# First batch's keys and values loaded by tokens and pooled in four quadrants, scaled in the copy

## The chip, the cores and the metric

One core of a Trainium2 chip runs the whole program. The metric is the device time of one execution in microseconds (us). Three runs of the kernel before took 746.22, 747.27 and 748.57 us; the median is 747.27 us. Five engines work side by side, each through its own instructions in a fixed order: TensorE (PE; its weight loads are listed as PEld), VectorE (DVE), ScalarE (ACT), GpSimd (POOL) and SyncE (SP), which here only issues DMA transfers. They wait for each other through semaphores.

## What is computed

Memory attention over 4 batches, 8 heads, 576 tokens, 64 numbers a head and 32 memory slots, and two feed-forward layers behind it on the 2304 tokens:

```python
a = np.exp(phi - np.max(phi, axis=2, keepdims=True))
a = a / (np.sum(a, axis=2, keepdims=True) + 1e-09)        # over the 576 tokens
k_m = np.einsum('bhsm,bhsd->bhmd', a, k)                   # pooled keys, 32 a head
v_m = np.einsum('bhsm,bhsd->bhmd', a, v)                   # pooled values
scores = np.matmul(q, k_m.transpose(0, 1, 3, 2)) / np.sqrt(64)
attn = softmax(scores)                                     # over the 32 slots, with 1e-09
x = np.matmul(attn, v_m)                                   # then heads side by side: 2304 x 512
x = (x @ w_a) * (x @ w_b) @ w_out                          # 512 -> 1536 -> 512
h = x @ w2_in
return np.maximum(0.01 * h, h) @ w2_out                    # 512 -> 2048 -> 512
```

## The kernel before, in words

The pooled values are never multiplied with the attention by themselves. Instead v_m is multiplied with a piece of w_a and w_b (`plan_w`, TensorE line L1195, written to the PSUM tile `wp`), the result is split into a high and a low part W (ACT L1220, DVE L1224), and the attention AT, also split (ACT L1135, DVE L1139), is multiplied with W in three passes (`plan_ab`, L1257, tile `ab`). ACT copies the a half (L1274), DVE multiplies it with the b half (L1279), the product G is split (L1294, L1298), and `plan_x1` multiplies it with w_out (L1323, tile `x1p`). Such a unit of work covers one batch and six of the twelve 128-wide column blocks f; there are eight units, four batches with f 0 to 5, then four with f 6 to 11. The second layer (lines L1761 and above, tiles `h` and `o`) starts when all is done, and its code and order are untouched by the change.

The weights arrive as 64-bit-like words through `stage` tiles, and each load of 512 KB is converted by ACT and POOL or ACT (L436, L440, L444) and joined by DVE (L454); w_out takes two more steps (ACT L462, DVE L465).

Batch 0 stands at the head of the program, where nothing can cover it. Its steps: maximum and exponential of phi into e; the pooling of keys and then values (`pool_pairs`, L754, 36 multiplications each, tile `km`); the sums of e over tokens (`total`, L799), their inverse r (L808, L809); the inverse spread to rows (`to_rows`, L816, and copies L826, L838); the pooled block copied out (L856, L859) and turned (`mem_t`, L870, tile `kvT`); the turned keys multiplied with the rows into kk (L886), the turned values multiplied with the rows into vblk (L894); queries turned (L1026, L982); the scores (L1062, L1068); and the softmax on DVE and ACT (row maximum L1005, subtraction L1014, exponential L1091, row sums L1100, inverse L1107, product L1112). The result is turned (L1122) and split into AT. Small multiplications without use (`warm`, L1691) keep TensorE at work in the gaps of the first 27 us.

The pooling of the keys multiplies, for token row j, the lower and the upper 64 partitions (g) with the heads of one half (a):

```python
out=km0[64 * a:64 * a + 64, g, 128 * n:128 * n + 128],
lhsT=c["e"][rows, j, 2 * a:2 * a + 2].rearrange("p q m -> p (q m)"),
rhs=c["kv", a][rows, :, n, D * j:D * j + D],
```

The order of all instructions up to the second layer comes from a planner (`Plan`): every step has an engine, a cost, the steps it waits for and a latest time, and the planner runs through the steps engine by engine, always taking the most urgent one that can start. A table of numbers (`SEEDS`) then shifts the latest times of randomly drawn steps, one draw for each number. So a change in a step's cost, in what it waits for, or in the table can move instructions anywhere up to the second layer. The ranks in `first` fix the order of the first twelve loads on SP.

Of the kernel before, what the change touches and what calls it, by code (L numbers as in the profile page):

```python
# [46 lines left out]
class Plan:  # L47
# [14 lines left out]
    SEEDS = (732418, 598209, 67790, 750449, 735046, 463859, 81198, 743086, 257381, 567596, 473366, 451655, 673169,  # L62
             737747, 770024, 60013, 601371, 972463, 52455, 949269, 18998, 526698, 544420, 584452, 460089, 892981,
             534221, 902381, 581733, 954758, 270819, 973106, 531934, 82330, 738265, 747344, 546437, 989455, 690754)
# [272 lines left out]
def kernel(  # L337
# [182 lines left out]
    att_all = []  # L520
# [8 lines left out]
    def plan_att(b):  # L529
# [15 lines left out]
        kv_slots = ((kv_before, kv_users), (early_end() if b >= B - 2 else [], []))  # L545
# [12 lines left out]
        for n, (name, src) in enumerate((("k", k), ("v", v))):  # L558
            ld_kv.append([])
            for i in range(2):  # L560
                part = slice(2 * i, 2 * i + 2)

                def load_kv(n=n, i=i, part=part, src=src):
# [5 lines left out]
                late = 0.5 if b == 0 and n and not i else 0.0  # L569
                ld_kv[n].append(add(DMA, 1.5 + late, load_kv, kv_slots[i][0], uses=[kv_slots[i][1]]))  # L570
# [94 lines left out]
        if b == 0:  # L665
# [23 lines left out]
            for i in range(2):  # L689

                def part_sum(i=i):
                    e = c["e"]
                    x = e[:, NR:] if i else e[:, 0:3]
                    dve.tensor_tensor(out=e[:, NR:], in0=x, in1=e[:, 3 * i + 3:3 * i + 6], op=ALU.add)

                s_es.append(add(DVE, t_dve(384), part_sum, s_exp[:i + 2] + s_es, port=True, uses=[e_users]))
        else:
            es_before, es_users = plan.slot("mx")
        for i in range(2 if b else 0):
# [17 lines left out]
            def part_sum(i=i):  # L717
# [5 lines left out]
                )  # L723

        for i in range(2 if b else 0):
            s_es.append(add(
                DVE, t_dve(384), lambda i=i: part_sum(i), s_exp + s_es + es_before, port=True, uses=[phi_users, es_users]
            ))
# [20 lines left out]
        def pool_pairs(n, a, j0, j1):  # L749

            for j in range(j0, j1):
                for g in range(NG):
                    rows = slice(D * g, D * g + D)
                    pe.matmul(  # L754
                        out=km0[64 * a:64 * a + 64, g, 128 * n:128 * n + 128],
                        lhsT=c["e"][rows, j, 2 * a:2 * a + 2].rearrange("p q m -> p (q m)"),
                        rhs=c["kv", a][rows, :, n, D * j:D * j + D],
                        start=j == 0, stop=j == NR - 1, skip_group_check=True,
                    )

        if b == 0:
            s_pool = []
            for n in range(2):
                end = []
                for a in range(2):
                    for i, (j0, j1) in enumerate(thirds):
                        end.append(add(
                            PE, POOL2 / 40 * NG * (j1 - j0), lambda n=n, a=a, j0=j0, j1=j1: pool_pairs(n, a, j0, j1),
                            [s_exp[i], ld_kv[n][a]] + sum(s_pool, []) + end[-1:] + r_before,
                            uses=[e_users, kv_users], n=4 * NG * (j1 - j0), kind="f",  # L770
                        ))
# [9 lines left out]
        if b == 0:  # L781
            t0_before = [plan.slot("t0", 2) for _ in range(NG)]
            t1_before, t1_users = plan.slot("t1")
            s_r, s_rv = [], []
            rm_before, rm_users = plan.slot(f"G{FH - 1}")

            def rows_place():
                c["rm"] = keep.tile([128, NG, NQ, 2, M], F32, tag=f"G{FH - 1}", name="rows")
                nc.gpsimd.memset(c["rm"], 0.0)

            s_rm = add(POOL, 0.5, rows_place, rm_before, uses=[rm_users])
            rv_before, rv_users = plan.slot("kmn")
            r_before, r_users = plan.slot("r")
            hold = Hold("ab", 2 + NG)
# [1235 lines left out]
```

## Time and profile before

| | |
|---|---|
| median of three runs | 747.27 us |
| the profiled execution | 745.72 us, of which 743.6 us are the span of its instructions |
| TensorE busy | 735.3 us, 99% of the span |
| VectorE, ScalarE, GpSimd busy | 579.3, 415.4, 17.9 us |
| first product of AT and W | starts 30.02 us into the span |
| second layer | first multiplication at 388.24 us |
| granted TensorE clock | nine tenths of full speed or more in all of the 40 slices |

The profiled execution was 1.55 us faster than the median of the runs. TensorE's busy time counts an instruction from its start to its modelled end, so a full share says that it always had something in it, and not that it did useful work: the fillers of the head count as busy. DMA share 1.00 and above means that all 16 transfer engines had work all the time.

### The profile page before, as it was taken

The numbers are of one execution on the slowest core, as the hardware profiler recorded it, in microseconds if no ns is written. First come the engines' busy times: TensorE is split into PE (matmuls) and PEld (weight loads), VectorE is DVE, ScalarE is ACT, GpSimd is POOL, SyncE is SP. The second block draws the span as 40 slices with busy tenths as digits, with TensorE's granted clock in tenths as the row PEclk, the third lists the DMA queues.
The fourth block names the chain that finished last, engine by engine and source line by source line (L and its number), as shares of the span: only waits on it lengthen the run. The fifth ranks groups of instructions, "written<-read, shape, count | busy, mean of one in ns | idle before, by whom it ended". The sixth has DMA issues, their size and how long they took to land.

```text
span 743.6 us, 14566 instructions
## 1 busy us (share of the span) xinstructions
PE 735.3 (99%) x5409; PEld 660.1 (89%) x5409; DVE 579.3 (78%) x1192; ACT 415.4 (56%) x917; POOL 17.9 (2%) x33
## 2 busy tenths in 40 slices
PE   9999999999999999999999999999999999999997
PEld 6798897987988888887999999999999999999986
DVE  5897685957917899998746766998866997877796
ACT  3786774765739687765514454644444743454441
POOL 1110000000300000000000000000000000000000
PEclk9999999999999999999999999999999999999999
DMA  9995366472804888777547787788898777878583
GB/s 313 352 370 177 106 242 215 156 238 77 268 7 165 270 319 301 253 258 284 194 161 227 264 247 256 253 254 251 256 299 285 262 250 244 280 226 312 150 301 86
DMA packets 86918, 175.28 MB, mean 236 GB/s; under 512 B 8000, under 2 KB 35136, under 8 KB 86848
## 3 DMA queue, kind: packets, MB, share of 16 engines
q1 hardware_dynamic: 86128, 173.77, 70.3%
q8 instruction: 43, 0.70, 0.4%
q10 hardware_dynamic: 720, 0.59, 0.3%
q14 instruction: 27, 0.22, 0.1%
HBM read 140.25 MB, written 34.08 MB: 234 GB/s over the span
## 4 chain that ended last, share of the span: by engine, by line
PE 96%; DVE 2%; DMA 1%; issue 0%; ACT 0%; SPq 0%
PE h L1761 24%; PE ab L1257 21%; PE x1p L1323 18%; PE o L1861 15%; PE o L1865 8%; PE wp L1195 3%; PE warm L1691 1%; PE km L754 1%; DMA stage<-in_moe_w_out_dram 1%; PE qT L1026 1%; PE sc L1062 1%; PE km L742 1%; PE aT L1122 1%; PE h L1836 0%; DVE s L1112 0%
## 5 line engine op out<-in xcount | busy, mean ns | idle before, releaser
L1861 PE MATMUL o<-w2o,S 128*128 128x512 f32 (+1 forms) x504 | 177.1, 387 | 0.0
L1257 PEld LDWEIGHTS ab<-AT,W 128*128 128x128 f32 x1152 | 154.6, 188 | 9.3 <-ACT W L1220 5.6
L1257 PE MATMUL ab<-AT,W 128*128 128x288 f32 x1152 | 160.8, 298 | 1.5 <-DVE W L1224 1.0
L1323 PE MATMUL x1p<-G,wo 128*128 128x512 f32 (+1 forms) x720 | 155.4, 371 | 0.3 <-DVE r L914 0.3
L1813 ACT ACTIVATE S<-g 128x384 fp32r<-128x384 f32 x168 | 87.6, 523 | 99.5 <-PE o L1861 86.0
L1323 PEld LDWEIGHTS x1p<-G,wo 128*128 128x128 f32 x720 | 123.7, 189 | 21.6 <-DVE r L914 0.6
L1761 PE MATMUL h<-T,ring 128*128 128x384 f32 x720 | 141.8, 335 | 0.0
L1865 PE MATMUL o<-w2o,S 128*128 128x256 f32 x492 | 137.6, 280 | 0.0
L1761 PEld LDWEIGHTS h<-T,ring 128*128 128x128 f32 x720 | 120.9, 188 | 4.1
L1814 DVE TENSOR_TENSOR S<-g,S 128x384 fp32r<-128x384 f32 x168 | 91.4, 553 | 40.4 <-ACT S L1813 40.2
L1861 PEld LDWEIGHTS o<-w2o,S 128*128 128x128 f32 x504 | 93.7, 188 | 14.6
L1865 PEld LDWEIGHTS o<-w2o,S 128*128 128x128 f32 x492 | 92.8, 189 | 0.0
L1883 DVE TENSOR_TENSOR C<-C,o 128x768 f32<-128x768 f32 x75 | 71.0, 948 | 13.9 <-ACT C L1887 7.9
L1761 PE MATMUL h<-B,ring 128*128 128x384 f32 x288 | 57.2, 336 | 0.0
L1804 DVE TENSOR_TENSOR g<-g 128x384 f32<-128x384 f32 x96 | 52.2, 552 | 2.9 <-ACT g L1771 2.4
L1761 PEld LDWEIGHTS h<-B,ring 128*128 128x128 f32 x288 | 48.8, 188 | 1.6
L436 ACT ACTIVATE stage<-stage 128x512 f32<-128x512 f32 x68 | 46.1, 683 | 4.1 <-DMA stage<-in_moe_w_in_dram 3.1
L1274 ACT COPY a_sb<-ab 128x288 f32<-128x288 f32 x96 | 37.3, 398 | 13.9 <-PE ab L1257 13.2
L1279 DVE TENSOR_TENSOR g<-a_sb,ab 128x288 f32<-128x288 f32 x96 | 42.3, 447 | 2.9 <-PE ab L1257 1.4
L1224 DVE TENSOR_TENSOR W<-wp,W 128x256 fp32r<-128x256 f32 (+1 forms) x75 | 35.1, 493 | 8.4 <-ACT W L1220 7.7
L1298 DVE TENSOR_TENSOR G<-g,G 128x576 fp32r<-128x576 f32 x48 | 37.1, 772 | 3.8 <-ACT G L1294 3.1
L1294 ACT ACTIVATE G<-g 128x576 fp32r<-128x576 f32 x48 | 33.1, 690 | 9.7 <-DVE g L1279 9.4
(146 smaller groups left out, 743.3 us busy)
## 6 DMA issues: line engine op xcount, KB each, us to landing
w2o<-a_scr SPq DMA_DIRECT2D x168, 256.0 KB, 3.7
ring<-a_scr SPq DMA_DIRECT2D x72, 512.0 KB, 4.4
stage<-in_moe_w_out_dram SPq DMA_DIRECT2D x28, 512.0 KB, 4.8
a_scr<-w2o SPq DMA_DIRECT2D x24, 512.0 KB, 4.4
a_scr<-a_out SPq DMA_DIRECT2D x24, 512.0 KB, 4.8
stage<-in_moe_w_in_dram SPq DMA_DIRECT2D x16, 512.0 KB, 5.2
stage<-in_moe_w_a_dram SPq DMA_DIRECT2D x12, 512.0 KB, 8.2
stage<-in_moe_w_b_dram SPq DMA_DIRECT2D x12, 512.0 KB, 8.2
```

Source lines behind the costliest of these rows:

```text
L436: act.activation(out=x, in_=x, func=ACTF.Prelu, scale=2.0 ** -112, alpha=2.0 ** 32)
L1257: pe.matmul(out=c[x, n][:, :HS], lhsT=W[b, f][:, hw, g, 128 * x:128 * x + 128], rhs=AT[b][:, g, ha, n * HS:(n + 1) * HS], start=(g == 0 an ...
L1274: act.copy(c["sb"][:, n], c[0, n][:, :HS])
L1279: dve.tensor_tensor(out=c["g"][:, n], in0=c["sb"][:, n], in1=c[1, n][:, :HS], op=ALU.mult)
L1323: pe.matmul(out=c["ps"], lhsT=wo_t[f][:, hw, 128 * m:128 * m + 128], rhs=G[f][:, hg, first:first + n], start=(f == fs[0] and (hw, hg) == P ...
L1761: pe.matmul(out=out, lhsT=ring[i % 2, part][:, o, kp, hw], rhs=x[:, hx], start=fresh and kp == 0 and (hw, hx) == PASSES[0], stop=kp == 1 a ...
L1804: dve.tensor_tensor(out=t, in0=x, in1=y, op=op)
L1813: act.activation(out=t[:, 0], in_=src, func=ACTF.Copy)
L1814: dve.tensor_tensor(out=t[:, 1], in0=src, in1=t[:, 0].bitcast(F32), op=ALU.subtract)
L1861: pe.matmul(out=dst[:, u, :y - x], lhsT=hi, rhs=wide[:, x:y], start=fresh and x == 0, stop=False, skip_group_check=True,)
L1865: pe.matmul(out=dst[:, u, :256], lhsT=lo, rhs=t[:, 0], start=False, stop=q == 3, skip_group_check=True,)
L1883: o_adds.append(lambda x=x: dve.tensor_tensor(out=total[name], in0=total[name], in1=x, op=ALU.add))
```

## The change

For batch 0, a load of keys or values used to bring two of the four head pairs with all nine token rows; it now brings all four head pairs with six token rows first (768 KB) and three after (384 KB). The pooling goes through all four quadrants (halves of heads a, halves of partitions g) for each token row. The second load of w for f 0 is put ahead of the values. DVE adds the three partial sums to one row, for all batches, so that the multiplication that sums over partitions is one in place of three. For batch 0, the inverse is no longer spread to rows: the copy of the pooled block scales with r, kk is multiplied with a mask of zeros and ones that POOL writes at the start, and vblk becomes a copy. `plan_w_parts` makes the products of a W whose halves lie in two banks wait for both halves in the plan (but for the first W). The table `SEEDS` has 53 numbers in place of 39.

```diff
-    SEEDS = (732418, 598209, 67790, 750449, 735046, 463859, 81198, 743086, 257381, 567596, 473366, 451655, 673169,
+    SEEDS = (683652, 560159, 530175, 125177, 433488, 159828, 165231, 686446, 405802, 158260, 349165, 253408, 67255,
...
+                def load_all(n=n, i=i, src=src):
+                    if ("kv", n) not in c:
+                        pool, tag = (keep, "AT1") if n else (p_att, "kv")
+                        c["kv", n] = pool.tile([128, NQ, NR * D], F32, tag=tag, name="kv_t")
+                    x = slice(6 * D * i, 6 * D + 3 * D * i)
+                    dma.dma_start(out=c["kv", n][:, :, x], in_=flat(src)[:, :, x])
...
-                late = 0.5 if b == 0 and n and not i else 0.0
-                ld_kv[n].append(add(DMA, 1.5 + late, load_kv, kv_slots[i][0], uses=[kv_slots[i][1]]))
+                if b == 0:
+                    late = 0.5 if n and not i else 0.0
+                    ld_kv[n].append(add(DMA, (2.0, 1.05)[i] + late, load_all))
+                else:
+                    ld_kv[n].append(add(DMA, 1.5, load_kv, kv_slots[i][0], uses=[kv_slots[i][1]]))
...
+                for j in range(1, 1 + 2 * i):
+                    dve.tensor_tensor(out=es[:, 0], in0=es[:, 0], in1=es[:, j], op=ALU.add)
...
             for j in range(j0, j1):
-                for g in range(NG):
-                    rows = slice(D * g, D * g + D)
-                    pe.matmul(
-                        out=km0[64 * a:64 * a + 64, g, 128 * n:128 * n + 128],
-                        lhsT=c["e"][rows, j, 2 * a:2 * a + 2].rearrange("p q m -> p (q m)"),
-                        rhs=c["kv", a][rows, :, n, D * j:D * j + D],
-                        start=j == 0, stop=j == NR - 1, skip_group_check=True,
-                    )
+                for a in range(2):
+                    for g in range(NG):
+                        rows = slice(D * g, D * g + D)
+                        pe.matmul(
+                            out=km0[64 * a:64 * a + 64, g, 128 * n:128 * n + 128],
+                            lhsT=c["e"][rows, j, 2 * a:2 * a + 2].rearrange("p q m -> p (q m)"),
+                            rhs=c["kv", n][rows, 2 * a:2 * a + 2, D * j:D * j + D],
+                            start=j == 0, stop=j == NR - 1, skip_group_check=True,
+                        )
...
-                for j in range(3):
-                    pe.matmul(
-                        out=c["sum"][:, :NG], lhsT=c["e"][:, NR + j].rearrange("p q m -> p (q m)"), rhs=ones,
-                        start=j == 0, stop=j == 2,
-                    )
...
+                pe.matmul(
+                    out=c["sum"][:, :NG], lhsT=c["e"][:, NR].rearrange("p q m -> p (q m)"), rhs=ones, start=True, stop=True
+                )
...
+                    for i in range(NG if n else 1):
+                        src = km0[:, g + i, 128 * n:128 * n + 128].rearrange("p (u d) -> p u d", u=2)
+                        dst = t[:, :, i] if n else t
+                        src = src if n else src.unsqueeze(2).to_broadcast([128, 2, 2, D])
+                        scale = c["r"][:, 1, g + i:g + i + 1]
+                        if on == ACT:
+                            act.activation(out=dst, in_=src, func=ACTF.Copy, scale=scale)
+                        else:
+                            dve.tensor_scalar(out=dst, in0=src, scalar1=scale, scalar2=None, op0=ALU.mult)
...
-                        dve.tensor_tensor(out=kk[g], in0=src, in1=c["rm"][:, g], op=ALU.mult)
+                        dve.tensor_tensor(out=kk[g], in0=src, in1=c["mask"], op=ALU.mult)
...
-                        dve.tensor_tensor(out=vblk[b], in0=c["kvT", 0, 1], in1=c["rv"], op=ALU.mult)
+                    def values(copy):
+                        copy(vblk[b], c["kvT", 0, 1])
...
-            for g in range(NG) if wide else (k,):
-                w_end[b, f, g] = [hi, lo]
+            ends = [hi, lo] if k == 0 or (b, f) == (0, 0) else ends + [hi, lo]
+            for g in (k,) if (b, f) == (0, 0) else range(NG):
+                w_end[b, f, g] = ends
...
-        ("wab", 0, 0), ("v", 0, 0), ("wab", 0, 1), ("v", 0, 1), ("wab", 1, 0), ("wab", 1, 1),
+        ("wab", 0, 0), ("wab", 0, 1), ("v", 0, 0), ("v", 0, 1), ("wab", 1, 0), ("wab", 1, 1),
```

The lines of the changed kernel have other numbers: L754 becomes L771, L799 L814, L870 L858, L1026 L1014, L982 L970, L1195 L1183, L1257 L1246, L1323 L1312, and ACT's L436, L856 and L1220 become L438, L844 and L1208.

On TensorE, from the pooling of the keys (`km`) to the last step ahead of the scores, before:

```order
L754 MATMUL km<-kv_t,e 64x128 x30
L799 MATMUL sum<-ones,e 128x2 x3
L754 MATMUL km<-kv_t,e 64x128 x6
L1026 MATMUL qT<-ident,q_t 128x128 x4
L816 MATMUL sum<-ident,r 128x128 x2
L870 MATMUL kvT<-ident,kc 128x2x32 x4
L982 MATMUL qL<-ident,q_t 128x128 x2
L1026 MATMUL qT<-ident,q_t 128x128 x8
```

and now:

```order
L771 MATMUL km<-kv_t,e 64x128 x36
L814 MATMUL sum<-ones,e 128x2
L1014 MATMUL qT<-ident,q_t 128x128 x4
L858 MATMUL kvT<-ident,kc 128x2x32 x4
L1014 MATMUL qT<-ident,q_t 128x128 x4
L970 MATMUL qL<-ident,q_t 128x128 x2
L1014 MATMUL qT<-ident,q_t 128x128 x4
L970 MATMUL qL<-ident,q_t 128x128 x2
```

The sums stand behind all of the pooling, the two multiplications that spread r are gone, and twelve turns of queries stand between the turned keys (kvT) and the first score, all of the second queries' among them.

On ScalarE, from the copy of the pooled values (kc) to the first attention parts (AT), before; `stage` is the conversion of a weight load:

```order
L856 COPY kc<-km 128x256
L440 ACTIVATE stage<-stage 128x512
L436 ACTIVATE stage<-stage 128x512
L440 ACTIVATE stage<-stage 128x512
L436 ACTIVATE stage<-stage 128x512
L1135 ACTIVATE AT<-aT 128x3x2x64
L1220 ACTIVATE W<-wp 128x256 x2
L1135 ACTIVATE AT<-aT 128x3x2x64 x2
```

and now:

```order
L844 ACTIVATE kc<-km,r 128x2x64 x2
L438 ACTIVATE stage<-stage 128x512
L882 COPY vblk<-kvT 128x128
L438 ACTIVATE stage<-stage 128x512
L1208 ACTIVATE W<-wp 128x256 x2
L1123 ACTIVATE AT<-aT 128x3x2x64 x2
```

ScalarE now makes vblk itself, between the conversions of the two weight loads for f 1 (the second waits for the load of w_b), and the first W and all of AT stand behind that second conversion.

On TensorE in the first unit, from the second pair's W products (`wp`) on; `ab` are products of AT and W, `x1p` those of G and w_out, `km` the pooling of batch 1. Before:

```order
L1195 MATMUL wp<-wab,vblk 32x512 x8
L625 MATMUL mxT<-ident,mx 128x128
L1257 MATMUL ab<-AT,W 128x288 x3
L1026 MATMUL qT<-ident,q_t 128x128 x4
L1257 MATMUL ab<-AT,W 128x288 x6
L655 MATMUL bc<-ident,gx 128x128
L1257 MATMUL ab<-AT,W 128x288 x30
L982 MATMUL qL<-ident,q_t 128x128 x4
L1257 MATMUL ab<-AT,W 128x288 x15
L1026 MATMUL qT<-ident,q_t 128x128 x4
L1257 MATMUL ab<-AT,W 128x288 x3
L1323 MATMUL x1p<-G,wo 128x512 x3
```

and now:

```order
L1183 MATMUL wp<-wab,vblk 32x512 x8
L970 MATMUL qL<-ident,q_t 128x128 x4
L1246 MATMUL ab<-AT,W 128x288 x3
L1312 MATMUL x1p<-G,wo 128x512 x3
L1246 MATMUL ab<-AT,W 128x288 x6
L1014 MATMUL qT<-ident,q_t 128x128 x4
L1246 MATMUL ab<-AT,W 128x288 x12
L1014 MATMUL qT<-ident,q_t 128x128 x4
L1246 MATMUL ab<-AT,W 128x288 x12
L1312 MATMUL x1p<-G,wo 128x512 x3
```

The first product with w_out used to stand behind all 144 products of AT and W of this unit; now 48 of them (6, 12, 12, and 18 more further down) stand behind it.

On SP, seven loads of batch 1 (keys twice, values once, queries twice, phi twice) stood ahead of the first load of w_out; now only one of phi does. The twelve loads of w_a and w_b for f 0 to 5 stand ahead of it in both.

## Rows read from the trace of the kernel before

**Rows 1.** The page: the span, and the chain that ended last, by engine.
```profile
span 743.6 us, 14566 instructions
...
PE 96%; DVE 2%; DMA 1%; issue 0%; ACT 0%; SPq 0%
```

**Rows 2.** Timeline of TensorE's head: start us, us, engine, line, what, count, [idle before].
```profile
8.46 3.12 PE L754 MATMUL km<-kv_t,e 64*64 64x128 f32 x60
...
13.78 1.00 PE L870 MATMUL kvT<-ident,kc 128*128 128x64 f32 x8
...
16.15 0.73 PE L1062 MATMUL sc<-kk,qT 128*64 128x64 f32 x16
...
22.87 2.18 PE L754 MATMUL km<-kv_t,e 64*64 64x128 f32 x36
...
27.51 1.20 PE L1122 MATMUL aT<-ident,s 128*128 128x128 f32 x9 [0.24 <-DVE s L1112]
...
30.02 5.32 PE L1257 MATMUL ab<-AT,W 128*128 128x288 f32 x36
```

**Rows 3.** Timeline of TensorE: pooling and sums of batch 1, W products of batch 3.
```profile
53.67 0.85 PE L1323 MATMUL x1p<-G,wo 128*128 128x512 f32 x3
54.45 2.25 PE L742 MATMUL km<-kv_t,phi_t 64*32 64x128 f32 x144
56.63 0.83 PE L906 MATMUL km<-ones,es 128*128 128x2 f32 x6
57.32 2.30 PE L1323 MATMUL x1p<-G,wo 128*128 128x512 f32 x9
...
176.34 2.81 PE L1195 MATMUL wp<-wab,vblk 64*32 64x512 f32 x48
```

**Rows 4.** Timeline of VectorE in the head, and its first w_out block.
```profile
12.37 0.16 DVE L808 TENSOR_SCALAR r<-sum 128x2 f32<-128x2 f32 x1 [2.46 <-PE sum L799]
...
26.22 0.29 DVE L894 TENSOR_TENSOR vblk<-kvT,rows 128x128 f32<-128x128 f32 x1 [1.58 <-PE kvT L870]
26.43 1.02 DVE L1112 TENSOR_TENSOR s<-s,m 128x576 f32<-128x576 f32 x1
...
52.75 0.78 DVE L465 TENSOR_TENSOR wo<-stage,wo 128x512 fp32r<-128x512 f32 x1
```

**Rows 5.** Timeline of ScalarE ahead of the first W.
```profile
25.10 0.37 ACT L856 COPY kc<-km 128x256 f32<-128x256 f32 x1 [2.30 <-PE km L754]
...
25.93 0.65 ACT L436 ACTIVATE stage<-stage 128x512 f32<-128x512 f32 x1
...
28.48 0.65 ACT L1220 ACTIVATE W<-wp 128x256 fp32r<-128x256 f32 x2
29.00 0.89 ACT L1135 ACTIVATE AT<-aT 128x384 fp32r<-128x384 f32 x2
```

**Rows 6.** Timeline of SP: issues of the last V load, one w_b, the first w_out.
```profile
6.83 3.28 SPq L567 DMA_DIRECT2D kv_t<-in_v_dram  x1
...
10.77 2.82 SPq L429 DMA_DIRECT2D stage<-in_moe_w_b_dram  x1
...
35.56 2.22 SPq L429 DMA_DIRECT2D stage<-in_moe_w_out_dram  x2
```

**Rows 7.** DMA issues at 6.8, 10.7 and 35.5 us: count, KB, us from issue to landing.
```profile
kv_t<-in_v_dram SPq DMA_DIRECT2D x1, 576.0 KB, 13.4
...
stage<-in_moe_w_b_dram SPq DMA_DIRECT2D x1, 512.0 KB, 12.5
...
stage<-in_moe_w_out_dram SPq DMA_DIRECT2D x1, 512.0 KB, 9.8
```

**Rows 8.** Windows: stretch, length, busy time by engine, PE clock, DMA share, GB/s.
```profile
30.37:54.45 24.08, 24.08 (x194) 21.31 (x193) 22.44 (x42) 21.03 (x44) 3.92 (x5) 1.00 1.03 378
```

**Rows 9.** TensorE's waits over all the span, and the last unit's first wait.
```profile
PE ab L1257 <- DVE W L1224: 1.0, 2, 0.5
...
337.77 0.53 PE L1257 MATMUL ab<-AT,W 128*128 128x288 f32 x2 [0.52 <-ACT W L1220]
```

More of the change, by code (lines that the diff above doesn't have):

```diff
@@ L723, in part_sum @@
                 )
+                for j in range(1, 1 + 2 * i):
+                    dve.tensor_tensor(out=es[:, 0], in0=es[:, 0], in1=es[:, j], op=ALU.add)
         for i in range(2 if b else 0):
             s_es.append(add(
-                DVE, t_dve(384), lambda i=i: part_sum(i), s_exp + s_es + es_before, port=True, uses=[phi_users, es_users]
+                DVE, t_dve(384) + 2 * i * t_dve(128), lambda i=i: part_sum(i), s_exp + s_es + es_before, port=True, uses=[phi_users, es_users]
             ))
@@ L764, in plan_att @@
                 end = []
[L765 to L771, printed above, removed]
+                for i, (j0, j1) in enumerate(thirds):
+                    end.append(add(
+                        PE, POOL2 / 40 * 2 * NG * (j1 - j0), lambda n=n, j0=j0, j1=j1: pool_pairs(n, j0, j1),
+                        [s_exp[i], ld_kv[n][i // 2]] + sum(s_pool, []) + end[-1:] + r_before,
+                        uses=[e_users, v_users if n else kv_users], n=8 * NG * (j1 - j0), kind="f",
+                    ))
                 s_pool.append(end)
@@ L809, in inverse @@
                 dve.reciprocal(out=r[:, 1], in_=r[:, 0])
[L811 to L843 removed]
+            s_inv = add(DVE, 0.2, inverse, s_sum[-1:] + r_before, give=[hold], uses=[r_users])
         hold_v = Hold("ab", 1)
@@ L849, in plan_att, with blocks @@
                 before, kc_users = (t1_before, t1_users) if n else t0_before[g]
-                def blocks(copy, g=g, n=n):
+                def blocks(on, g=g, n=n):
                     t = c["kc", g, n] = keep.tile(
@@ L885, in keys @@
                         src = c["kvT", g, 0].unsqueeze(2).to_broadcast([128, NQ, 2, M])
-                        dve.tensor_tensor(out=kk[g], in0=src, in1=c["rm"][:, g], op=ALU.mult)
+                        dve.tensor_tensor(out=kk[g], in0=src, in1=c["mask"], op=ALU.mult)
                     s_kk.append(add(
-                        DVE, t_dve(256), keys, [s_kvt, *s_r] + before, give=[hold_t], uses=[users, rm_users]
+                        DVE, t_dve(256), keys, [s_kvt, s_rm] + before, give=[hold_t], uses=[users, rm_users]
                     ))
                 else:
-                    def values():
-                        dve.tensor_tensor(out=vblk[b], in0=c["kvT", 0, 1], in1=c["rv"], op=ALU.mult)
+                    def values(copy):
+                        copy(vblk[b], c["kvT", 0, 1])
                     vb_end[b, 0] = vb_end[b, 1] = add(
-                        DVE, t_dve(128), values, [s_kvt, *s_rv], give=[hold_v], uses=[rv_users]
+                        DVE, t_dve(128), lambda values=values: values(dve.tensor_copy), [s_kvt], give=[hold_v],
+                        other=[(ACT, 0.2, lambda values=values: values(act.copy))],
                     )
@@ L904, in total @@
             def total():
-                for j in range(3):
-                    pe.matmul(
-                        out=c["km", 0][:, 128:128 + NG], lhsT=c["es"][:, j].rearrange("p q m -> p (q m)"), rhs=ones,
-                        start=j == 0, stop=j == 2,
-                    )
+                pe.matmul(
+                    out=c["km", 0][:, 128:128 + NG], lhsT=c["es"][:, 0].rearrange("p q m -> p (q m)"), rhs=ones,
+                    start=True, stop=True,
+                )
             def inverse():
```

66 lines of the change are left out of this document (17 added, 49 removed), and 4 rows, old and new, of the table SEEDS.

## The prediction

> **What bounds the kernel now.** I read the page first. The chain that ended last is 96% TensorE [rows 1], so the kernel gets faster only where TensorE has less to do, stands still less, or starts its useful work earlier. Then I read TensorE's timeline from the start: until the first product of attention and W at 30.02 us [rows 2] it turns, pools and fills; from there on it has work without a break. The views of waits and windows say where the rest may hide: all waits of those products (ab) for W together are 1.0 + 0.5 = 1.5 us, in the last unit [rows 9], while between 30 and 54 us DVE is busy 22.44 and ACT 21.03 of 24.08 us with all transfer engines at work (share 1.03) [rows 8]. So there are four questions: how much earlier does ab start, what do the sums save, what becomes of the 1.5 us, and can loads and conversions follow if ab starts earlier.
>
> **The head.** Three chains end at ab's start.
>
> *Keys to scores.* The price of a pooling multiplication is the first step. Before, 30 of them (60 records) took 3.12 us, 0.104 each [rows 2]. A full-size turn with as many columns (aT, nine in 1.20 us) costs 0.13 with its tail, so two multiplications on different partition halves, but the same half of heads, did not overlap. Multiplications that differ in the columns they fill do overlap: batch 1's pooling on four column groups needs 2.25/72 = 0.031 each, and 24 W products with 512 columns need 2.81/24 = 0.117, where four times the columns of a 0.104 would be 0.42 [rows 3]. That is a gain of about 3.4 to 3.6 for four column groups; the quadrants give two. I take half, 0.055; the ends are 0.104 (no overlap) and 0.031.
>
> The Trainium skill, TensorEngine Tiling (Array Packing), section Tiling Modes, says that different tiles can load weights and multiply in parallel. By that rule the two partition halves would have overlapped already, at about 0.052, and four quadrants would give 0.026; the rows at 0.104 speak against the rule for these halves. The sum by 0.026 would be the same, since a load decides below, but the disagreement is why I keep a chance for no overlap at all.
>
> The first load of keys is a third larger, and 192 KB at 378 GB/s [rows 8] are 0.5 us, so pooling starts at about 9.0 in place of 8.46 [rows 2] and ends at 9.0 + 36 x 0.055 = 11.0. The sum is now one multiplication, 0.83/3 = 0.3 [rows 3]; the two small operations for r are 0.16 each [rows 4], the copy 0.37 [rows 5], and the gaps some 0.2: the turn (kvT) starts at about 12.2 in place of 13.78 [rows 2]. The two further DVE additions lie in a stretch in which DVE waited 2.46 us [rows 4] and cost nothing. kk no longer waits for rows. Twelve turns of queries now stand ahead of the first score: 12.2 + 1.0 + 12 x 0.13 = 14.8, against 16.15 [rows 2]. From the first score to the end of the second product with 1/sum took 27.45 - 16.15 = 11.3 us; 1.58 of that was DVE waiting for the turned values and 0.29 the vblk operation [rows 4], which ACT now has. So 9.4 remain, and the softmax ends at about 24.2 in place of 27.45.
>
> *Values to W.* The last load of values has the same bytes ahead of it and landed at 6.83 + 13.4 = 20.2 [rows 6, 7]. Then 12 multiplications at 0.055 follow in place of the 18 that ran from 22.87 for 2.18 us [rows 2]: 20.9; two scaled copies at no more than 0.37 each [rows 5], 21.7; turn and copy about 1.0, 22.7. Before it was 26.51 [rows 4].
>
> *What is late next.* On ACT the first W stands behind the conversion of f 1's w_b. That load landed at 10.77 + 12.5 = 23.3 [rows 6, 7] and has no fewer bytes ahead of it now. Conversion 0.65, two W copies 0.65, two AT copies 0.89 [rows 5], and the low parts on DVE behind them (about 1.2): 26.7. So ab starts at 26.7, and the head gains 30.02 - 26.7 = 3.3 us. With pooling at 0.104 the scores begin 1.8 us later, the softmax ends at 26.0, and with the 2.6 us that lay between its end and ab before, ab starts at 28.6: a gain of 1.4. With pooling at 0.031 nothing changes, the load decides. If the load lands a little sooner, 3.7.
>
> **The sums of batches 1 to 3.** Three multiplications took 57.32 - 56.63 = 0.69 us of TensorE's time [rows 3]; one should take 0.25 to 0.35. I take 0.4 saved, three times, 1.2 (0.6 to 1.4). The added DVE operations (two of 128 columns a batch, about 0.3 each) come before the pooling of their batch ends, so TensorE does not wait for them; uncovered they would cost 3 x 0.6.
>
> **Whole W.** It concerns only W in two banks; the plan may now put other work where TensorE stood 1.5 us [rows 9]. In the unit that stood, though, the order now puts all 144 ab behind the W products without x1p between. I take 0.5 gained, between 1.5 gained and 1.5 lost.
>
> **Catching up.** ab uses up weights 3.3 us earlier, with DVE and ACT 93% and 87% busy and the transfer engines full [rows 8]. The plan loads all w_a and w_b of the first unit ahead of batch 1's keys and values, which helps; the joins of f 3 still need loads that land near 29 us (four loads behind 23.3, 1.4 us each at 378 GB/s), when ab reaches their W products at about 32 (26.7 + 36 x 5.32/36, [rows 2]). I take 0.8 lost (0 to 3.3, the whole head).
>
> **Sum.** -3.3 - 1.2 - 0.5 + 0.8 = -4.2 us, on 745.72 us profiled: 741.5. The median of the runs was 1.55 us above that execution, so the forecast for the median is 743.0.
>
> **Rivals.**
> 1. *The quadrants don't overlap.* For it: the 0.104 [rows 2]. Against: the W products and batch 1's pooling [rows 3]. Head 1.4 in place of 3.3: -2.3, 745.0.
> 2. *The head is given back.* The loads set the pace from 27 to 54 us, and TensorE waits there for what it gained. For it: the share of 1.03 [rows 8]. Against: before, TensorE never stood in that stretch, so there was some slack. Catching up costs 3.3: -1.7, 745.6.
> 3. *The first x1p comes too early* (slower). Before, the first product with w_out ran at 53.67 behind all 144 ab, and its block was ready at 53.5, 8.1 us after its load landed at 35.56 + 9.8 = 45.4 [rows 3, 4, 6, 7]. Now it stands with 48 ab behind it, and TensorE reaches it after 96 ab, 16 W products and a turn of queries: 26.7 + 96 x 5.32/36 [rows 2] + 16 x 0.117 [rows 3] + 0.5 = 43.3. For it: the full transfer engines, and DVE at 93% [rows 8]. Against: the load now has about 3.2 MB less ahead of it (two loads of keys, one of values, two of queries, one of phi), 8.6 us at 378 GB/s, so it lands near 37, and an urgent conversion of five operations takes 3 to 4 us: 41. If the load were no earlier and the conversion no quicker, TensorE would stand from 43.3 to 53.5, 10.2 us; half of that, and 1.7 more of the waits of rival 2, give -4.2 + 6.8 = +2.6, 749.9, which I take as its price. It decides from a block later than 43.3; it makes the kernel slower from about 47.5 on.
>
> **How the numbers follow.** Forecast 0.62, first rival 0.11, second 0.17, third 0.10. What a measurement of this kernel can tell from no change is about 0.3%, 2.2 us; so faster means below 745.0, slower above 749.5. The forecast is faster but for a few cases in a hundred, the first rival half faster and half the same, the second mostly the same, the third two thirds slower: faster 0.70, the same 0.22, slower 0.08. The likeliest case's own range is 741 to 745, from the bounds of the sums and of whole W. The range for 8 in 10 reaches from 740.3 (sums 1.4, whole W 1.5, head 3.7, nothing lost, less what seldom comes together) over the first two rivals to 747.3.
>
> **What would show it.** In the profile of the changed kernel: the 72 pooling multiplications at about 0.055 each (rival 1: 0.1); kvT of the keys at 12.2 and the first score at 14.8; the first W on ACT right behind a conversion that ended at about 24; ab's first instruction at 26.7; the sums of batches 1 to 3 at 0.25 to 0.35 each; no wait of x1p L1312 ahead of 50 us (rival 3) and less than 1 us of ab's waits there (rival 2); the second layer's first multiplication at about 384 in place of 388.24. The prediction is wrong if ab starts before 27.5 and the second layer does not start before 386.5, or if pooling is as slow as before.

## The result and the profile after

The changed kernel takes 739.34 us (median of 4 runs, 739.13 to 739.49), the kernel before 747.32 us beside it: a ratio of 0.9893, 95% interval 0.9875 to 0.991. The change gains 8.0 us; 4.2 were forecast, and the time lies below the range. The profiled execution took 739.38 us (before 745.72), so here profile and median agree, where before they lay 1.6 us apart. That difference turns out to be part of the answer.

First the page: span, and the chain that ended last, by engine.

```profile
span 737.6 us, 14546 instructions
...
PE 92%; DVE 4%; ACT 2%; DMA 1%; issue 1%; SPq 0%; DVEq 0%; ACTq 0%
```

TensorE still bounds the kernel, as in [rows 1]. Then its timeline (start us, us, engine, line, what, count, [idle before]), with the lines that answer to [rows 2, 3, 9] and the last unit.

```profile
9.31 2.20 PE L771 MATMUL km<-kv_t,e 64*64 64x128 f32 x72 [0.35 <-DMA kv_t<-in_k_dram]
...
12.85 1.24 PE L858 MATMUL kvT<-ident,kc 128*128 128x64 f32 x8 [0.32 <-ACT kc L844]
...
15.57 0.69 PE L1050 MATMUL sc<-kk,qT 128*64 128x64 f32 x16
...
18.90 1.56 PE L1680 MATMUL warm<-const-float32-1.0 128*128 128x512 f32 x4
20.39 2.19 PE L771 MATMUL km<-kv_t,e 64*64 64x128 f32 x72
...
25.01 1.20 PE L1110 MATMUL aT<-ident,s 128*128 128x128 f32 x9
...
27.50 3.13 PE L1246 MATMUL ab<-AT,W 128*128 128x288 f32 x20
...
43.89 0.86 PE L1312 MATMUL x1p<-G,wo 128*128 128x512 f32 x3
...
57.50 2.25 PE L758 MATMUL km<-kv_t,phi_t 64*32 64x128 f32 x144
59.67 0.38 PE L894 MATMUL km<-ones,es 128*128 128x2 f32 x2
59.92 2.33 PE L1312 MATMUL x1p<-G,wo 128*128 128x512 f32 x9
...
325.80 10.13 PE L1312 MATMUL x1p<-G,wo 128*128 128x512 f32 x44
335.86 2.81 PE L1183 MATMUL wp<-wab,vblk 64*32 64x512 f32 x48
338.60 5.58 PE L1246 MATMUL ab<-AT,W 128*128 128x288 f32 x40
...
382.81 2.24 PE L1750 MATMUL h<-B,ring 128*128 128x384 f32 x12
```

The pooling of the keys takes 2.20 us for all 36 multiplications, where 30 took 3.12; ab starts at 27.50 in place of 30.02; one sum holds TensorE for 59.92 - 59.67 = 0.25 us in place of 0.69; the first x1p (43.89) has no wait; the last unit's ab follows its W products at once, where before there were three waits of 0.5; the second layer starts 5.43 us sooner. What was pooled last, the first W, and the first W of the last unit, on ScalarE:

```profile
22.66 0.63 ACT L844 ACTIVATE kc<-km,r 128x128 f32<-128x128 f32 x2 [1.32 <-PE km L771]
...
24.19 0.69 ACT L438 ACTIVATE stage<-stage 128x512 f32<-128x512 f32 x1
25.17 0.66 ACT L1208 ACTIVATE W<-wp 128x256 fp32r<-128x256 f32 x2 [0.28 <-PE wp L1183]
...
337.04 1.26 ACT L1208 ACTIVATE W<-wp 128x256 fp32r<-128x256 f32 x4 [1.76 <-PE wp L1183]
```

The first W does stand behind a conversion, but waits for its own product, made from values that came late. In the last unit (337.04) ScalarE is idle and takes W as soon as its products allow.

**Where the time came from.** The two orders place x1p differently, so I compare starts with equal work behind them (44 x1p take 10.13 us, 0.23 each). At ab's start the gain is 2.52 us. At batch 1's pooling it is 54.45 - (57.50 - 21 x 0.23) = 1.8. The three sums add 1.3. At the last unit's W products it is 334.45 + 21 x 0.23 - 335.86 = 3.4, so 0.3 came from places in between. At the second layer it is 5.4: the last unit gave 2.0. The second layer was 0.6 shorter in these two profiles, but its length is 354.7 to 355.0 us in the other profiles of both kernels; that part is scatter.

### The profile page after: what moved, and what is told of

Its sections match the earlier page's. It is cut to its first block, busy times and chain, and to the rows that moved or that the text cites. A ratio compares the mean times of both kernels' runs of the same rounds, so it can differ in the third digit from the quotient of the medians.

```text
span 737.6 us, 14546 instructions
## 1 busy us (share of the span) xinstructions
PE 730.4 (99%) x5391; PEld 654.5 (89%) x5391; DVE 579.7 (79%) x1196; ACT 414.0 (56%) x915; POOL 20.0 (3%) x38
## 4 chain that ended last, share of the span: by engine, by line
PE 92%; DVE 4%; ACT 2%; DMA 1%; issue 1%; SPq 0%; DVEq 0%; ACTq 0%
PE h L1750 24%; PE x1p L1312 19%; PE ab L1246 18%; PE o L1850 15%; PE o L1854 8%; PE wp L1183 3%; DMA kv_t<-in_k_dram 1%; PE sc L1050 1%; PE qT L1014 1%; DVE G L1287 1%; PE km L771 1%; PE km L758 1%; DVE g L1268 0%; DVE W L1212 0%; PE aT L1110 0%
## 5 line engine op out<-in xcount | busy, mean ns | idle before, releaser
L1246 PEld LDWEIGHTS ab<-AT,W 128*128 128x128 f32 x1152 | 154.8, 188 | 7.2 <-ACT W L1208 2.5
L1246 PE MATMUL ab<-AT,W 128*128 128x288 f32 x1152 | 160.0, 297 | 0.5 <-DVE W L1212 0.3
L1312 PE MATMUL x1p<-G,wo 128*128 128x512 f32 (+1 forms) x720 | 156.6, 372 | 0.0
L1312 PEld LDWEIGHTS x1p<-G,wo 128*128 128x128 f32 x720 | 123.5, 189 | 22.3 <-issue 0.8
L438 ACT ACTIVATE stage<-stage 128x512 f32<-128x512 f32 x68 | 45.7, 683 | 4.9 <-DMA stage<-in_moe_w_in_dram 2.7
```

Of the source, the lines that this page charges most:

```text
L438: act.activation(out=x, in_=x, func=ACTF.Prelu, scale=2.0 ** -112, alpha=2.0 ** 32)
L1246: pe.matmul(out=c[x, n][:, :HS], lhsT=W[b, f][:, hw, g, 128 * x:128 * x + 128], rhs=AT[b][:, g, ha, n * HS:(n + 1) * HS], start=(g == 0 an ...
L1312: pe.matmul(out=c["ps"], lhsT=wo_t[f][:, hw, 128 * m:128 * m + 128], rhs=G[f][:, hg, first:first + n], start=(f == fs[0] and (hw, hg) == P ...
```

## Experiments

**The kernel before again.** No edit.

> The kernel before, unchanged, timed and profiled once more. Theory A (the last unit's stall depends on when a weight load lands, and so differs between executions): the waits of ab for W at 337 to 340 us add up to something else than the 1.5 us of the first profile, by as much as this execution differs from 745.7 us. Theory B (what lies between 745.72 us profiled and the median of 747.3 is spread over the program): the stall is 1.5 us again within 0.2, and the places where the two traces part are elsewhere, each below 0.5 us.

It took 746.98 us (744.42 to 749.25, 12 runs). The profiled execution took 747.17 us. Theory A fell: it is 1.45 us longer than the first, and its waits for W in the last unit are 1.3 us, 0.2 less. Of theory B only that holds: the traces part by far the most at one place. TensorE's timeline there, in the first profile of the kernel before:

```profile
156.65 0.48 PE L1323 MATMUL x1p<-G,wo 128*128 128x512 f32 x1
157.41 2.10 PE L1323 MATMUL x1p<-G,wo 128*128 128x512 f32 x8 [0.27 <-DVE r L914]
```

and in this one:

```profile
156.24 0.47 PE L1323 MATMUL x1p<-G,wo 128*128 128x512 f32 x1
158.28 3.66 PE L1323 MATMUL x1p<-G,wo 128*128 128x512 f32 x8 [1.56 <-issue]
```

Behind batch 3's pooling TensorE stands 1.56 us for nothing that the profile shows, and then the same eight products take 3.66 in place of 2.10. The windows of this execution (stretch, length, busy, clock, DMA share, GB/s) show more:

```profile
157.00:158.00 1.00, 0.00 (x0) 1.00 1.03 344
158.00:160.00 2.00, 1.72 (x4) 0.61 1.03 265
160.00:162.00 2.00, 2.00 (x7) 0.54 0.98 269
162.00:164.00 2.00, 2.00 (x14) 1.00 1.04 357
```

A microsecond without any TensorE work, then the granted clock at its lower level (1.2 GHz) for some 3 us, with the transfer engines full. Together they cost 2.85 us more than in the first profile (1.56 for 0.27, and 3.66 for 2.10). Every run lists its mean granted clock and span: of 75 executions of the kernel before in these experiments, 46 have 0.994 to 0.998 and a median span of 745.6 us, 29 have 0.999 or 1.0 and 743.1. Of 14 executions of the changed kernel 13 have 0.999 or 1.0, and the one at 0.998 is no longer than the rest; their median span is 737.5 us. The profile above is the only one of the 46. In 40 of them the mean clock is lower still than its 0.998, so they spent more time at the lower level than this stretch holds, and no trace shows where.

**W first in the last unit of before.** The order of emission alone (`parts` keeps the product and the copies of a W):

```diff
-        for step in plan.order(idle=(WARM, fillers)):
-            step.emit()
+        made = parts[B - 1, FH] + parts[B - 1, FH + 1][1:]; order = plan.order(idle=(WARM, fillers)); i = max(i for i, x in enumerate(order[:order.index(made[0])]) if x.engine == PE) + 1; order = [x for x in order[:i] if x not in made] + made + [x for x in order[i:] if x not in made]
+        for step in order: step.emit()
```

> The kernel before, with ScalarE's and VectorE's four parts of W of the last unit (f 6 and 7 of batch 3) moved ahead of the weight conversions that stood before them; nothing else moves. Theory A: TensorE's three waits for W at 337 to 340 us (0.52, 0.47, 0.50) go, the later conversions are early enough, the second layer starts 1.4 to 1.6 us sooner: -1.5 us, and the runs scatter less than the 2.3 us of the kernel before. Theory B (the stall is given back because the conversions, 1.2 us later, hold up the products with w_out): no change, within 0.5 us, with a wait of x1p behind them.

745.69 us against 747.08: -1.4 us, theory A. The ratio on record, which here and below is not that of the two medians, is 0.9971 (0.9955 to 0.9988). ScalarE before, where W (L1220) stood behind conversions that waited for a load of w_out:

```profile
335.86 0.72 ACT L436 ACTIVATE stage<-stage 128x512 f32<-128x512 f32 x1 [1.01 <-DMA stage<-in_moe_w_out_dram]
336.48 0.68 ACT L440 ACTIVATE stage<-stage 128x512 int32<-128x512 uint32 x1
...
337.37 0.90 ACT L1220 ACTIVATE W<-wp 128x256 fp32r<-128x256 f32 x3
```

and with the edit:

```profile
335.34 0.66 ACT L1220 ACTIVATE W<-wp 128x256 fp32r<-128x256 f32 x2 [0.76 <-PE wp L1195]
336.22 0.72 ACT L1220 ACTIVATE W<-wp 128x256 fp32r<-128x256 f32 x2 [0.22 <-DVE W L1224]
336.83 0.66 ACT L436 ACTIVATE stage<-stage 128x512 f32<-128x512 f32 x1
```

TensorE's timeline with the edit:

```profile
334.16 2.81 PE L1195 MATMUL wp<-wab,vblk 64*32 64x512 f32 x48
336.90 1.46 PE L1257 MATMUL ab<-AT,W 128*128 128x288 f32 x9
...
386.21 2.25 PE L1761 MATMUL h<-B,ring 128*128 128x384 f32 x12
```

From W products to second layer 52.05 us, where before had 388.24 - 334.45 = 53.79 and the changed kernel has, at equal work, 382.81 - 335.86 + 4.83 = 51.78. So nearly all of the last unit's 2.0 us is this stall. The runs still scatter (743.3 to 746.9): half of them have a mean granted clock of 0.998 or less, as before.

**The changed kernel without the rule on whole W.**

```diff
-            ends = [hi, lo] if k == 0 or (b, f) == (0, 0) else ends + [hi, lo]
-            for g in (k,) if (b, f) == (0, 0) else range(NG):
+            ends = [hi, lo]
+            for g in range(NG) if wide else (k,):
                 w_end[b, f, g] = ends
```

> The changed kernel without the rule that products wait in the plan for both halves of W; the table stays, and the plan puts much else in another order from 47 us on. Read at the last unit: theory A (the rule takes the stall away): ab waits for W there again, 1 to 1.5 us, as before. Theory B (the order that the table happens to give takes it away): no wait above 0.3 us there. The total is not forecast closely: 738 to 744 us, since the table was drawn for another plan.

744.63 us (744.05 to 745.79), just above the 738 to 744 that I expected. The plan differs in many places, so the 5.3 us are not the rule's price. But its timeline of TensorE answers the question:

```profile
92.79 0.79 PE L1246 MATMUL ab<-AT,W 128*128 128x288 f32 x4 [1.51 <-DVE W L1212]
...
341.01 2.81 PE L1183 MATMUL wp<-wab,vblk 64*32 64x512 f32 x48
343.75 8.50 PE L1246 MATMUL ab<-AT,W 128*128 128x288 f32 x62
```

Without the rule a wait for W of 1.5 us comes back, but in the second unit; the last unit has none. Theory B holds for that place: the order that the table gives there has no stall, with the rule or without. What the rule itself is worth was not measured.

**The order of the pooling.** First in short runs (a third of the pooling goes through one half of the heads, then the other):

```diff
-            for j in range(j0, j1):
-                for a in range(2):
+            for a in range(2):
+                for j in range(j0, j1):
```

> The changed kernel, where each third of the pooling of batch 0 runs through one half of the heads first and then the other, so that only the two partition halves alternate, as before. Theory A (multiplications that fill other columns overlap, those on the other partition half alone do not): 0.104 us each in place of 0.061, so 3.7 us for 36 in place of 2.20, the first score 1.5 us later, ab's start near 29.0 in place of 27.5, and +1.0 to +1.5 us: 740.1 to 740.6. Theory B (the price comes from the load of 64 rows and columns as such, whatever the order): 2.2 us, no change, 739.1.

740.36 us (739.28 to 741.34), within theory A's range by the total but not by its steps: both poolings take 2.46 us, as TensorE's timeline shows.

```profile
9.20 2.46 PE L771 MATMUL km<-kv_t,e 64*64 64x128 f32 x72
```

Runs of six cost only 0.27 us a pooling. So the next one has long runs of 18:

```diff
...
+            for j, a, g in [] if j1 < NR else [(j, a, g) for u in range(2) for j in range(NR)
+                                               for v in range(2) for g, a in [(v, u) if n else (u, v)]]:
...
```

> A measurement of the pooling's price by itself, in the changed kernel: all 36 multiplications of a pooling stand in one piece (behind all of its loads), the keys' in two runs of 18 in which only the halves of the heads alternate, the values' in two runs of 18 in which only the partition halves alternate (before's order, in longer runs than the 6 of the last experiment). Theory A (quadrants work side by side; runs of 6 were short enough for the next quadrant's to start before the last one's ended): both near 3.7 us for 72 records, 0.10 a multiplication, with a faster stretch where the half changes. Theory B (before's 0.104 came from something else, such as the layout of the load): the values' stay at 2.2 to 2.5 us. The total is not of interest, the keys start later.

Theory A. TensorE's timeline, keys (column halves alternate) and values (partition halves alternate):

```profile
8.76 3.77 PE L771 MATMUL km<-kv_t,e 64*64 64x128 f32 x72 [0.21 <-ACT e L698]
...
21.42 3.77 PE L771 MATMUL km<-kv_t,e 64*64 64x128 f32 x72
```

Windows of the values' pooling:

```profile
22.50:23.00 0.50, 0.50 (x15) 1.00 1.10 348
23.00:23.50 0.50, 0.50 (x21) 1.00 1.11 350
23.50:24.00 0.50, 0.50 (x16) 1.00 1.19 365
```

0.105 a multiplication with two quadrants in use, whichever pair, and 0.061 with four; it is faster only where the half changes (21 records). I read this as queued work of the next quadrants that starts while the last ones' runs, which would also be why runs of six hid the difference. The gain is the quadrants', not the load's layout.

**Three sums again** in the changed kernel (the same edit in batch 0, and VectorE's two additions left out):

```diff
-                pe.matmul(
-                    out=c["km", 0][:, 128:128 + NG], lhsT=c["es"][:, 0]...
+                for j in range(3):
+                    pe.matmul(
+                        out=c["km", 0][:, 128:128 + NG], lhsT=c["es"][:, j]...
```

> The changed kernel with the sums over tokens in three multiplications again, and without VectorE's two further additions, in all four batches. Theory A (batches 1 to 3 pay 0.44 each, as the profiles show 0.69 against 0.25 from the sums to the next product; batch 0 pays about 0.4 ahead of its scores): +1.3 to +1.7 us, 740.4 to 740.8. Theory B (TensorE's time there is covered by what the next products wait for): below +0.5.

741.92 us (741.39 to 743.43), about 2.5 above the changed kernel and more than the 740.4 to 740.8 expected. TensorE's timeline:

```profile
10.01 2.20 PE L767 MATMUL km<-kv_t,e 64*64 64x128 f32 x72 [1.01 <-DMA kv_t<-in_k_dram]
...
60.75 0.83 PE L893 MATMUL km<-ones,es 128*128 128x2 f32 x6
61.44 0.93 PE L1311 MATMUL x1p<-G,wo 128*128 128x512 f32 x3
...
156.29 0.49 PE L893 MATMUL km<-ones,es 128*128 128x2 f32 x3 [0.52 <-issue]
```

Each sum costs 0.69 in place of 0.25, as theory A says (1.3 for three, 0.3 in batch 0). The rest of this profile, the slowest of the six runs (span 740.4 us), is a load of keys that came 0.7 us later, and 0.5 us of the stand seen above, now inside the sums: the pooling had moved from 151.3 to 153.1 us.

**Without the two fillers ahead of the values.**

```diff
     def warm(n):
+        if warmed.append(n) or len(warmed) in (7, 8): return
```

> The changed kernel without the two small multiplications without use (512 and 256 columns, four records, 1.56 us) that stand on TensorE between the last score at 18.9 us and the pooling of the values. Theory A (they, and not the load, hold the first two thirds of the pooling, whose load landed at 18.4): 24 multiplications run at 18.9 to 20.4, the last 12 end near 21.1 in place of 22.6, kc at 21.3, the first W about 1 us sooner, and ab starts at 26.5 to 26.9 in place of 27.5: -0.6 to -1.0 us, 738.3 to 738.7. Theory B (the conversion of f 1's w_b, which landed near 22.7, holds the first W on ScalarE anyway, or what is gained is given back by 54 us): ab within 0.3 us of 27.5, no change. Theory C (TensorE's granted clock falls for want of work): slower.

738.56 us (738.04 to 739.71). TensorE's timeline:

```profile
18.70 2.20 PE L771 MATMUL km<-kv_t,e 64*64 64x128 f32 x72
...
23.86 1.20 PE L1110 MATMUL aT<-ident,s 128*128 128x128 f32 x9 [0.42 <-DVE s L1100]
...
26.02 5.43 PE L1246 MATMUL ab<-AT,W 128*128 128x288 f32 x36
```

Theory A, and more of it than expected: the pooling runs at 18.70, all of it, and ab starts at 26.02, 1.48 us sooner. What TensorE waits for ahead of it now is the softmax (aT waits 0.42 for s). The changed kernel itself ran beside it:

> The changed kernel, unchanged, timed and profiled once more: 739.3 us within 0.4, ab's start at 27.5 within 0.2, no wait for W at 338 us, a second layer within 0.2 us of the first profile's. If the second layer's length differs by more than that, the 0.6 us by which it was shorter than before is scatter between executions.

738.98 us (738.35 to 740.86), ab at 27.5, a second layer of 354.8 us as in the first profile. Both once more, on another chip:

> The changed kernel, unchanged, as the measure for the others on the same chip: 738.6 to 739.4 us, clocks of 0.999 and above.

> The changed kernel without the two fillers ahead of the pooled values, again beside the changed kernel itself: 0.4 to 1.3 us less than that (ab started 1.48 us sooner, the second layer 0.8 to 1.3 us sooner in the first profiles); if less than 0.3, the head's gain does not reach the end.

739.64 us (738.97 to 739.71, a little above what was expected) and 738.70 (737.51 to 739.99). Over all executions the changed kernel has a median of 739.35 us (14), the one without the fillers 738.6 (10): some 0.7 us of the 1.5 reach the end. It is the fastest version of the study; against the kernel before its ratios are 0.9878 (0.9852 to 0.9905) and 0.9888 (0.9868 to 0.9908), whose intervals overlap those of the changed kernel.

**The stand at 157 us.** Three experiments. In the kernel before, batch 3's pooling and sums (`pooled`) earlier in the order:

```diff
-        for step in plan.order(idle=(WARM, fillers)):
-            step.emit()
+        order = plan.order(idle=(WARM, fillers)); i = [i for i, x in enumerate(order[:order.index(pooled[0])]) if x.engine == PE][-2]
+        for step in order[:i] + pooled[:2] + [x for x in order[i:] if x not in pooled[:2]]: step.emit()
```

> The kernel before, with batch 3's pooling and sums moved ahead of the six products with w_out that stood in front of them (1.4 us); nothing else moves. Of 23 timed runs of the kernel before 12 had a mean granted clock of 0.994 to 0.998 and a span near 745.6 us, 11 one of 0.999 to 1.0 and 743.1 us. Theory A (in the first group TensorE stands 1.6 us at 156.7 us, right behind the 144 records of this pooling and while the transfer engines are full, and then works 3 us at half clock, as in the second profile; the pooling now ends 1.4 us nearer to the start of those transfers at 153 us): the low clocks become rare, the median falls from 747.1 to 745.6 to 746.2 us. Theory B (the low clocks come from elsewhere): half of the runs keep them, 746.9 to 747.3 us.

745.99 us beside 748.4; the ratio on record is 0.9981 (0.9967 to 0.9996). Low clocks in 3 of 12 runs against 13 of 18 of the kernel before on the same chip: theory A, though not by the way that I thought, since the pooling then waited 0.67 us for ScalarE and started no earlier. What moved is the work behind it: TensorE reaches the place of the stand 1.1 us later (table below). In the other direction, work added to the changed kernel ahead of that pooling:

```diff
-                for hw, hg in PASSES:
+                for i, (hw, hg) in enumerate([PASSES[0]] * (11 if (b, f, m) == (2, 0, 0) else 0) + list(PASSES)):
...
```

> The changed kernel with one product with w_out ahead of batch 3's pooling (its first pass) repeated 11 times, which changes no number: 2.5 us more of TensorE's work, so that the pooling stands near 153.9 us, as in the kernel before. Theory A (the pooling's instructions arrive by the same transfer engines as the loads that start at 153 to 154 us; late, they make TensorE stand and lose its clock): the packet of instructions that lands at 152.3 in the changed kernel lands behind 153.5, some of the runs show a granted clock of 0.998 or less and take up to 2.4 us more, and the median is 2.5 to 5 us above the changed kernel's. Theory B (before's low clocks have to do with something else that the change took away): +2.5 us, all clocks at 0.999 or above.

741.45 us (740.89 to 743.47), 1.8 above the changed kernel, with no stand and one clock of 0.998 in six: theory B by the outcome. But the packet with TensorE's next instructions (queue q8 of the page) came at 153.1 us, still ahead of the full transfers, so the condition of theory A did not arise. With 3 long multiplications in place of the 11:

```diff
+                for i in range(3 if (b, f, m) == (2, 0, 0) else 0):
+                    pe.matmul(out=c["ps"], lhsT=wo_t[f][:, 0, 128 * m:128 * m + 128].bitcast(F32),
+                              rhs=G[f][:, 0, first:first + n].bitcast(F32), start=True, stop=True)
```

> The changed kernel with three multiplications of 512 columns in full fp32 ahead of the first product with w_out before batch 3's pooling, on the same inputs and into the place that this product then clears: 2.6 us more of TensorE's work with 6 records where the last experiment had 22. Theory A (the instructions behind the pooling's first half come as one packet of 16 KB, asked for at a fixed place in the stream, and land late once the transfers at 153 to 154 us run): the packet lands at 154.6 us or later, TensorE stands behind the pooling in some executions, a third or more of the runs show a clock of 0.998 or less and 2 us more, and the runs scatter by 3 us or more. Theory B: the packet lands late and no run is disturbed, all within 1.5 us, about 2 us above the changed kernel's 739.6.

742.80 us (742.11 to 743.44, 6 runs), 1.35 above the last one for nearly the same work. Of theory A the late packet and the stand came, the low clocks and the scatter did not; of theory B the quiet clocks, but not the total. TensorE's timeline, from the three long multiplications (six records) on:

```profile
148.08 2.74 PE L1312 MATMUL x1p<-G,wo 128*128 128x512 f32 x6
...
155.93 1.84 PE L1314 MATMUL x1p<-G,wo 128*128 128x512 f32 x7
158.85 0.73 PE L1314 MATMUL x1p<-G,wo 128*128 128x512 f32 x2 [1.08 <-issue]
```

Its instruction packet, in the view of DMA queues from 156.50 to 156.75 us (packets, MB, share of 16 engines):

```profile
q8 instruction: 1, 0.02, 23.2%
```

| profile | pooling starts | packet, start to end | record 3521 ends | record 3522 starts | TensorE stands |
|---|---|---|---|---|---|
| changed kernel | 151.34 | 152.44 to 153.39 | 157.02 | 156.63 | no |
| 11 short multiplications | 153.49 | 153.12 to 154.81 | 156.62 | 156.24 | no |
| three sums again | 153.09 | 153.38 to 154.81 | 155.76 | 156.28 | 0.52 |
| before, first | 153.79 | 154.75 to 156.00 | 157.13 | 157.40 | 0.27 |
| before, W first | 153.68 | 154.61 to 155.84 | 157.03 | 157.31 | 0.29 |
| before, pooling earlier | 153.77 | 154.80 to 156.32 | 158.26 | 158.09 | no |
| before, second | 153.38 | 155.93 to 156.89 | 156.72 | 158.28 | 1.56 |
| 3 long multiplications | 153.51 | 156.57 to 157.50 | 157.77 | 158.85 | 1.08 |

The records are TensorE's in the trace, counted from the start: multiplications, weight loads and semaphore instructions. In all five profiles with a stand it lies between records 3521 and 3522, whatever the order has put there, and it ends 1.35 to 1.47 us after the packet. Where TensorE comes to that record later than this, it does not stand. So it is shown that a late packet of instructions makes TensorE stand here, and the 0.27 us that the profile puts down to VectorE's r, which had ended at 157.19, belong to it too. The fall of the clock behind the stand is not explained: it came with 1.56 us and not with 1.08, and no run of this last kernel has a clock below 0.999. Why the packet came at 154.75 in one execution of before and at 155.93 in another is open. The queue moved 42 packets and 0.69 MB, 16 KB each. The Trainium skill, Runtime: NRT & Kernel Launch, section Instruction fetch mechanics, says that an engine fetches its program in blocks of 16 KiB through a DMA queue of its own, a cost that is mostly hidden. The size agrees; in these rows it was hidden only where the packet ended 1.4 us or more before its first record was due.

## Why the prediction was wrong

- *From profile to median* failed. "The median of the runs was 1.55 us above that execution, so the forecast for the median is 743.0" carries over 1.55 us that the changed kernel does not pay. Before, 46 of 75 executions have a low clock and a span 2.5 us longer than the rest; the profile shown, at 0.999, was one without. The one of the 46 that was profiled lost its time in and behind the stand at 157 us, and moving the pooling there cut the low clocks from 13 of 18 to 3 of 12. That this place made all 46 slow is not shown. In the changed kernel the packet had ended 3.2 us before its first record was due, and its median is 0.04 below its profile. I never asked where the difference came from.
- *Whole W*: the term was mis-sized. "I take 0.5 gained" measured 2.0 at the last unit. I doubted it because 144 ab now follow the W products directly; but ScalarE reached W at once (337.04, right behind its products), since no conversion that waits for a load stood in front. Rows 9 had the stall and its releaser; its cause was one view further, on ScalarE.
- *The head* was right in parts, and too large. The keys' pooling (0.061 each, 0.055 forecast; kvT at 12.85 for 12.2, first score at 15.57 for 14.8) ran late by a load that was 0.3 us behind the forecast and by copies; the softmax ended at 23.98 (24.2). The step that failed is "Then 12 multiplications at 0.055 follow": the other 24, whose load had landed at 7.37 + 11.0 = 18.4, had not run by then, because 1.56 us of fillers stood in front of them in the order. So kc came at 22.66 and not at 20.9. ab started at 27.50 and not at 26.7; without the fillers it started at 26.02, so the load of w_b behind the 26.7 did not set it either.
- *Overlap.* The forecast of the size held, its reason did not. "A full-size turn with as many columns (aT, nine in 1.20 us) costs 0.13 with its tail, so two multiplications on different partition halves, but the same half of heads, did not overlap" sets a turn of one record against a multiplication of two (60 records for 30). Three multiplications of 512 columns on the whole array, six records, took 2.74 us in the last experiment; by that, 128 columns are some 0.11 us a record and 0.23 a multiplication (an estimate, tail included). Beside it the 0.105 of either pair is two quadrants side by side, and the 0.061 nearly four; a single quadrant was not measured. So [rows 2] gave rival 1 no support, and the 0.055 was right because four quadrants halve what two cost. The Trainium skill, TensorEngine Tiling (Array Packing), section Tiling Modes, says that different tiles can load weights and multiply in parallel. The 0.105 and 0.061 agree with it; the 0.052 and 0.026 that I worked out by it were half of what it gives here.
- *Catching up*, 0.8 lost: 2.52 at ab's start had become 1.8 at batch 1's pooling, 0.7 lost. *Sums*, 1.2: 1.3, at 0.25 each. The first x1p was reached at 43.89 (43.3) without a wait, so rival 3 did not come; nor did rivals 1 and 2.
- The small rest: 0.3 us in the units between, 0.3 outside the span (745.72 - 743.6 against 739.38 - 737.6), and the 0.6 us of the second layer, by which the first profile of before was long.

Against the median the miss is 3.7 us: 1.55 carried over, 1.5 of the last unit, 1.2 in the last line and 0.1 of the sums, less 0.7 by which head and catching up together fell short (1.8 for 2.5).

## What to carry to other kernels

Where the profiled execution and the median differ by more than the effect asked about, find the place first: the runs' granted clocks and a second profile pointed to it in one step, and a change can remove it without meaning to. Look at what stands in order in front of a step on its own engine before timing it from its data, fillers included. And a wait's releaser is only the last link: read what that engine was doing just before.

## What was not expected of the hardware

- Instructions travel with the data: a 16 KB packet of TensorE's stream that came some 3 us later, among full transfers, left it standing 1.08 us, and in another execution 1.56 us with some 3 us at the lower clock behind. TensorE took up its next record 1.35 to 1.47 us after the packet had ended, in all five profiles with a stand.
- Quadrants need not alternate one by one: runs of three multiplications on each (six on a pair) took 2.46 us where strict alternation took 2.20 and runs of nine (18 on a pair) 3.77.
